# Block transposes by VectorE, gates on GpSimd and stores from ScalarE's queue in a fused chunk-selection attention and gated MLP kernel

## The chip, the cores and the metric

The kernel runs on one core of a Trainium2 chip. A core has five engines that run side by side, each through its own instruction list: TensorE (PE, matmuls; its weight loads are listed as PEld), VectorE (DVE), ScalarE (ACT), GpSimd (POOL) and SyncE (SP, here only the queue from which DMAs are issued). The metric is device microseconds for one execution: the median of three runs before the change is 215.47 us (215.21 to 215.66).

## What is computed

The reference is an attention that selects chunks of keys, followed by a gated MLP block that mixes tokens. Shapes: 4 batches, 8 heads, 768 tokens, head size 64; model width 512, inner width 1024.

```python
k_min, k_max = per-chunk min and max of k         # 24 chunks of 32 tokens
ub = sum_d max(q * k_min, q * k_max)              # bound of each query for each chunk
top_chunks = the 6 best chunks at or before the query's own
scores = q @ k.T / 8, kept where (j's chunk is in top_chunks) and j <= i
x = softmax(scores) @ v                           # [4, 768, 512], heads side by side
h = gelu(x @ w_in);  u, v = halves of h
v_n = layernorm(v) * g_ln
v_s = einsum('ts,bsd->btd', w_sg, v_n) + b_sg
out = x + (u * v_s) @ w_out
```

## The kernel before

**Pairs and batches.** Heads are worked in 16 pairs (pair p has heads 2p and 2p+1, four pairs to a batch). For each pair `prep` runs a K side, a q side, a V side and a selection; then come the scores with their exponentials, the products with V (`head`), and the transposed output (`xtrans`). When the fourth pair of a batch is done, `moe_h` and `moe_g` do the MLP for that batch, so that attention of later pairs and the MLP of an earlier batch lie in the same stretch of time.

**K side (`kside`, line 621).** `load_rows` (line 524) brings K of a pair as 128 tokens by 6 blocks by 2 heads by 64, two DMAs of 192 KB per tensor in runs of 256 B. TensorE transposes fp32 blocks of 128x128 against an identity (`rows_T`, line 545), six to a pair; VectorE reduces each transposed half to chunk minima and maxima straight from PSUM (line 643); ScalarE, and VectorE for pair 2, writes K as bf16 into `KA` (line 451). From pair 8 on (`KSPR`) both heads are written at once and two DMAs (lines 656 and 659) copy the second head to its own buffer and restore the mask rows there. GpSimd turns the maximum into maximum minus minimum (line 662).

**K side of pairs 12 to 15 (`kside2`, line 563, set `K2`).** GpSimd casts K to bf16 (line 572), two transposing DMAs write `KA` (line 576); VectorE transposes K in fp32 in blocks of 32x32 (line 579), reduces it (line 585), and every second pair regroups the results with 16 small copies (`regroup`, line 600). A transposing DMA and a copy ahead of pair 12 (`kb_init`, line 557) set up the constant rows.

**q side (`qside`, line 666).** Two groups of three fp32 transposes on TensorE, two evacuations into `qT` on ScalarE (VectorE for pairs 2 and 3), then on GpSimd the positive part (line 676) and bf16 casts into `QA` (line 683).

**Selection.** `select` (line 691) serves pairs 0 to 3, `select_full` (line 744) the later ones, two pairs at a time; `GROUPS` says which pairs go together. Small TensorE tiles give the bounds (lines 713 and 760), VectorE transposes them, takes the eight largest of each row, compares and transposes back. For later pairs four DMAs (line 793) put the result beside q.

**MLP.** `moe_h`: hidden products (lines 961 and 1007), GELU on ScalarE, batch statistics on VectorE, the power -1/2 of the variance on GpSimd (line 976), the normalization on VectorE (line 996). `moe_g`: token mixing on TensorE (line 1024), scale and bias on VectorE (line 1042), the gate product on VectorE (line 1046), the output matmul (line 1058), the residual (line 1066) and a store from SP's queue (line 1071) out of a ring of three buffers `osb`.

**Order.** Nothing is ordered at run time. `P.op` records each operation with its reads and writes; the table `TABLE` at the end lists, by operation number, the order in which each engine runs its operations and which PSUM slot each tile has; `link` derives the semaphore waits. A waiting instruction holds all that stands behind it on its engine, DMA issues among them.

## Time and profile before

| | |
|---|---|
| median of three runs | 215.47 us |
| span of the profiled execution, the only time that the profile gives for it | 216.2 us |
| VectorE busy | 187.7 us, 87% |
| ScalarE busy | 148.6 us, 69% |
| GpSimd busy | 106.1 us, 49% |
| DMA traffic | 36.26 MB, mean 168 GB/s |
| read from HBM, written | 24.77 MB, 6.29 MB |

The profile is of one execution. Busy times count the instructions that compute; issuing a DMA and waiting are not counted. Matmul ends are modelled, and overlapping matmuls are merged in busy time. A "chain" in the profile is followed back from the last instruction, at each step to what released it. Idle time of an engine matters only where another one waits for it.

### The profile page before, as it was taken

How to read it: one execution, taken by the hardware profiler on the slowest of the kernel's cores; microseconds unless marked ns; L12 is line 12 of the kernel's file. 1: busy time of each engine (PE TensorE's matmuls, PEld its weight loads, DVE VectorE, ACT ScalarE, POOL GpSimd, SP SyncE). 2: the span in 40 equal slices, each digit the busy share in tenths (PEclk: the TensorE clock that was granted, in tenths of full speed). 3: DMA queues.
4: the chain of work that ended last, by engine and by line, in shares of the span. 5: the costliest groups of instructions: out<-in, count | busy, mean ns of one | idle time of the engine just before them, and what ended most of it. 6: DMA issues, size and time to landing. Idle time of an engine off the chain costs nothing.

```text
span 216.2 us, 5890 instructions
## 1 busy us (share of the span) xinstructions
PE 199.7 (92%) x2292; PEld 133.3 (62%) x2307; DVE 187.7 (87%) x553; ACT 148.6 (69%) x223; POOL 106.1 (49%) x163
## 2 busy tenths in 40 slices
PE   7779998989999999999999997998796999999992
PEld 3547766745775668785466765875354686555650
DVE  3699997799999999998999999998997668788983
ACT  2768999847797597899478785998477597353000
POOL 7284669794539576655513936586531224011000
PEclk9999999999999999999999999999999799999998
DMA  7999999992789969948999899099731404501215
GB/s 153 219 219 180 245 326 234 346 289 63 167 224 236 203 149 245 209 122 195 227 184 204 203 172 263 22 183 199 155 60 40 112 0 40 181 0 53 97 75 216
DMA packets 95915, 36.26 MB, mean 168 GB/s; under 512 B 89488, under 2 KB 91024, under 8 KB 95888
## 3 DMA queue, kind: packets, MB, share of 16 engines
q1 hardware_dynamic: 95888, 35.89, 74.6%
q8 instruction: 18, 0.29, 0.6%
q14 instruction: 9, 0.07, 0.2%
HBM read 24.77 MB, written 6.29 MB: 144 GB/s over the span
## 4 chain that ended last, share of the span: by engine, by line
PE 74%; DVE 13%; ACT 5%; issue 2%; POOL 2%; DMA 2%; SPq 1%; DVEq 0%
PE PSG L1024 15%; PE PSC L834 11%; PE PSG L1058 8%; PE PSG L1007 7%; PE PSG L545 7%; PE PSG L961 6%; PE PSG L912 6%; PE PSG L760 3%; PE PSC L874 3%; DVE Wg L600 2%; PE PSG L919 2%; PE PSC L376 2%; DVE stats L970 2%; DMA out_dram<-osb 2%; PE PSC L880 2%
## 5 line engine op out<-in xcount | busy, mean ns | idle before, releaser
L840 ACT ACTIVATE E<-PSC 128x1024 bf16<-128x1024 f32 (+1 forms) x72 | 63.2, 921 | 14.5 <-PE PSC L834 13.5
L834 PE MATMUL PSC<-QA,KA 128*128 128x128 bf16 (+2 forms) x336 | 38.4, 248 | 2.5 <-ACT E L840 2.5
L1024 PE MATMUL PSG<-wsgT,vhat 128*128 128x384 bf16 x192 | 35.8, 334 | 0.2 <-DVE vhat L996 0.2
L683 POOL CAST QA<-qT 64x768 bf16<-64x768 f32 (+1 forms) x28 | 23.2, 835 | 16.8 <-ACT qT L451 12.3
L834 PEld LDWEIGHTS PSC<-QA,KA 128*128 128x128 bf16 x336 | 24.3, 99 | 11.0 <-ACT E L840 3.8
L845 POOL TENSOR_SCALAR_AFFINE_SELECT E<-E 128x768 bf16<-128x768 bf16 x24 | 20.6, 866 | 20.1 <-ACT E L840 20.0
L643 DVE TENSOR_REDUCE W<-PSG 128x12 f32<-128x384 f32 x48 | 24.3, 546 | 5.0 <-PE PSG L545 4.6
L1024 PEld LDWEIGHTS PSG<-wsgT,vhat 128*128 128x128 bf16 x192 | 18.5, 99 | 12.1 <-issue 0.8
L1012 ACT ACTIVATE uT<-PSG 128x384 bf16<-128x384 f32 x32 | 14.7, 491 | 15.5 <-PE PSG L1007 15.4
L1042 DVE SCALAR_TENSOR_TENSOR PSG<-PSG,glnT,bsgbc 128x384 f32<-128x384 f32 x32 | 19.5, 617 | 6.5 <-PE PSG L1024 6.2
L965 ACT ACTIVATE vgb<-PSG 128x512 f32<-128x512 f32 x24 | 14.0, 597 | 13.1 <-PE PSG L961 12.8
L1007 PE MATMUL PSG<-xT,winb 128*128 128x384 bf16 x128 | 22.8, 326 | 0.0
L961 PE MATMUL PSG<-winb,xT 128*128 128x512 bf16 x91 | 21.3, 379 | 1.4 <-DVE xT L454 1.1
L889 ACT ACTIVATE E<-PSC 128x1024 bf16<-128x1024 f32 (+1 forms) x24 | 20.7, 914 | 2.6 <-PE PSC L880 2.5
L1058 PE MATMUL PSG<-woutb,uT 128*128 128x512 bf16 (+1 forms) x90 | 21.8, 370 | 0.6
L912 PE MATMUL PSG<-vx,E 128*128 128x65 bf16 x480 | 20.0, 193 | 1.0 <-issue 0.8
L912 PEld LDWEIGHTS PSG<-vx,E 128*128 128x128 bf16 x480 | 17.7, 97 | 3.5 <-issue 1.1
L1066 DVE TENSOR_TENSOR osb<-PSG,XS 128x512 f32<-128x512 f32 (+1 forms) x25 | 16.2, 660 | 2.9 <-PE PSG L1058 1.6
L929 DVE TENSOR_TENSOR XS<-PSG,rden 128x384 bf16<-128x384 f32 x32 | 17.4, 551 | 0.5
L1046 DVE TENSOR_TENSOR uT<-PSG,uT 128x384 bf16<-128x384 f32 x32 | 17.2, 551 | 0.5
L451 ACT ACTIVATE qT<-PSG 128x384 f32<-128x384 f32 x28 | 13.6, 496 | 5.3 <-PE PSG L545 5.0
L1007 PEld LDWEIGHTS PSG<-xT,winb 128*128 128x128 bf16 x128 | 12.2, 98 | 8.1 <-ACT vgb L965 0.3
(93 smaller groups left out, 351.2 us busy)
## 6 DMA issues: line engine op xcount, KB each, us to landing
kn<-in_k_dram SPq DMA_DIRECT2D x32, 192.0 KB, 4.3
qn<-in_q_dram SPq DMA_DIRECT2D x32, 192.0 KB, 4.5
vn<-in_v_dram SPq DMA_DIRECT2D x16, 384.0 KB, 5.5
out_dram<-osb SPq DMA_DIRECT2D x23, 256.0 KB, 2.6
uT<-in_moe_w_sg_dram SPq DMA_DIRECT2D x4, 384.0 KB, 6.7
vgb<-in_moe_w_in_dram SPq DMA_DIRECT2D x3, 512.0 KB, 4.9
QA<-Dt SPq DMA_DIRECT2D x24, 36.0 KB, 2.0
vhat<-in_moe_w_sg_dram SPq DMA_DIRECT2D x2, 384.0 KB, 7.4
```

The lines of the kernel that those rows point to most:

```text
L643: P.op("dve", lambda d, m=m, op=op, src=src, h0=h0, h1=h1: d.tensor_reduce(W[w][:, m, 12 * h0:12 * h1].rearrange("p (h c) -> p h c", h=h1 ...
L683: P.op("pool", lambda g, i=i, r0=r0, r1=r1: g.tensor_copy(QA[w][i or 0][r0:r1, :], qT[r][r0:r1, :]), gps(S, 250 if i == 1 else 150), ("qca ...
L834: r = e.matmul(t.ap()[:, o:o + n], KA[w][i][:, 128 * kb:128 * kb + 128], QA[w][i][:, q0:q0 + n], start=True, stop=True)
L840: P.op("act", lambda e, t=t, c0=c0, c1=c1, i=i: e.activation(E[es][:, i, c0:c1], t.ap()[:, 0:c1 - c0], ACTF.Exp, scale=SCALE), act(c1 - c0 ...
L845: P.op("pool", lambda g, ev=ev: g.affine_select(ev, ev, pattern=[[0, NT], [1, 128]], compare_op=ALU.is_ge, fill=0.0, base=0, channel_multi ...
L889: P.op("act", lambda e, t=t, c0=c0, c1=c1, n=n: e.activation(E[es][:, :, c0:c1], t.ap().rearrange("p (i x) -> p i x", i=2)[:, :, 0:n], ACT ...
L912: r = e.matmul(t.ap()[:, 65 * qb:65 * qb + 65], E[es][:, i, a:a + 128], vx[w][:, kb, i, :], start=first, stop=False, skip_group_check=True)
L961: r = e.matmul(t.ap()[:, 0:F], xT[s][:, dk, 128 * qt:128 * qt + 128], winb[:, dk, F:DFF], start=(dk == 0), stop=(dk == NDK - 1))
L1007: r = e.matmul(t.ap()[:, 0:TG], winb[:, dk, 128 * fb:128 * fb + 128], xT[s][:, dk, TG * tg:TG * tg + TG], start=(dk == 0), stop=(dk == NDK ...
L1024: r = e.matmul(t.ap()[:, 0:TG], vhat[s][:, sb, 128 * fb:128 * fb + 128], wsgT[:, sb, TG * tg:TG * tg + TG], start=(sb == 0), stop=(sb == N ...
L1042: P.op("dve", lambda d, t=t, fb=fb, tg=tg: d.scalar_tensor_tensor(t.ap()[:, 0:TG], t.ap()[:, 0:TG], glnT[:, fb:fb + 1], bsgbc[:, TG * tg:T ...
L1058: r = e.matmul(t.ap()[:, 0:c1 - c0], gT[s][:, fb, 128 * qt:128 * qt + 128], woutb[:, fb, c0:c1], start=(fb == 0), stop=(fb == NF - 1))
```

## The change

- **K of pairs 8 to 15** (`KB`) and **q of pairs 9, 11, 13 and 15** (`QB`) are loaded by a new `load_slices`: four DMAs per tensor, one for each head and half of the head size, each onto 32 partitions in runs of 128 B, so that one VectorE transpose in blocks of 32x32 yields the transposed tensor as it is needed. For K that transpose goes to a scratch tile, from which VectorE takes minima and maxima of all 24 chunks, ScalarE copies the first head and VectorE the second head to `KA` as bf16 (`kblock`). For q it goes straight to `qT`. The set `K2` is empty, and with it go the transposing DMAs of K, the casts and the regrouping; for pairs 8 to 11 the copies of lines 656 and 659 go as well.
- **Gates** of batches 0, 1 and 2 (`GP`, all 24): VectorE writes scale and bias to SBUF in fp32 instead of back to PSUM, and GpSimd forms the product.
- **The power** is split in two halves of three token blocks (`RS = 2`).
- **Stores** of batches 0 to 2 are issued from ScalarE's queue (`STQ`); those of batch 3 stay on SP and come from the six buffers of `vgb` instead of the ring (`OSV`).
- **Selection**: pairs 2 and 3 form one group.
- **Order**: all lists of the table and the slots are written anew; matmuls that only keep TensorE warm at the start go from 12 to 7.

```diff
+    KB = (8, 9, 10, 11, 12, 13, 14, 15)
+    QB = (9, 11, 13, 15)
+    KBC = ("act", "dve")
...
+    RS = 2
+    STQ = (0, 1, 2)
...
+    OSV = (3,)
-    K2 = tuple(range(12, 16))
+    K2 = ()
...
-    GROUPS = [(0,), (1,), (2,), (3,)] + [(a, a + 1) for a in range(4, NP, 2)]
+    GROUPS = [(0,), (1,), (2, 3), (4, 5), (6, 7), (8, 9), (10, 11), (12, 13), (14, 15)]
...
+    def load_slices(p, nm, src, dst):
...
+        flat = dst[s][:].rearrange("p j i d -> p (j i d)").rearrange("p (c e) -> p c e", e=32)
+        for i in range(2):
+            for dh in range(2):
+                g = 2 * i + dh
+                o = P.op("sp", lambda e, i=i, dh=dh, g=g: e.dma_start(
+                    flat[32 * g:32 * g + 32], bass.AP(src.tensor, (2 * p + i) * S * DH + 32 * dh,
+                                                      [[DH, 32], [32 * DH, NC], [1, 32]])), dmac(),
...
+    def kblock(p):
...
+        P.op("dve", lambda d: d.transpose(KT, kn[s][:].rearrange("p j i d -> p (j i d)")), (865, 962), ("kbt", p),
+             reads=kr, writes=INDR)
+        for m, op in ((0, ALU.min), (1, ALU.max)):
+            P.op("dve", lambda d, m=m, op=op: d.tensor_reduce(
+                W[w][:, m, 0:NC], KT.rearrange("p (c x) -> p c x", x=32), axis=AX.X, op=op),
...
+            if KBC[i] == "act":
+                P.op("act", lambda e, i=i, r0=r0: e.activation(KA[w][i][r0:r0 + 64, :], KT[r0:r0 + 64, :], ACTF.Copy), (734, 845),
...
+        if p in QB:
+            P.op("dve", lambda d: d.transpose(qT[r][:], qn[s][:].rearrange("p j i d -> p (j i d)")), (865, 962), ("qbt", p),
...
+                if (b, k) in GP:
+                    xg = vgb[:, k % NT, 0:TG]
...
+                    P.op("dve", lambda d, t=t, fb=fb, tg=tg, xg=xg: d.scalar_tensor_tensor(
+                        xg, t.ap()[:, 0:TG], glnT[:, fb:fb + 1], bsgbc[:, TG * tg:TG * tg + TG],
...
+                    P.op("pool", lambda g, xg=xg, tg=tg, fb=fb: g.tensor_tensor(
+                        gT[s][:, fb, TG * tg:TG * tg + TG], xg, uT[s][:, fb, TG * tg:TG * tg + TG], op=ALU.mult),
...
-                    P.op("sp", lambda e, qt=qt, os_=os_, c0=c0, c1=c1: e.dma_start(
+                    P.op("act" if b in STQ else "sp", lambda e, qt=qt, ob=ob, c0=c0, c1=c1: e.dma_start(
```

## What was predicted before the changed kernel was run

> **What bounds the kernel now.** I read the page first, then the busy time by stretches, then the chain of waits, then the groups of instructions with shapes kept apart.
>
> ```profile
> span 216.2 us, 5890 instructions
> ...
> PE 199.7 (92%) x2292; PEld 133.3 (62%) x2307; DVE 187.7 (87%) x553; ACT 148.6 (69%) x223; POOL 106.1 (49%) x163
> ```
> ```profile
> 0.00:18.00 18.00, 14.33 (x121) 8.37 (x121) 12.15 (x44) 10.83 (x18) 9.93 (x26) 1.00 1.14 199
> 18.00:36.00 18.00, 17.90 (x349) 13.22 (x348) 16.88 (x57) 17.17 (x26) 13.18 (x20) 1.00 1.04 252
> 36.00:48.00 12.00, 10.09 (x185) 7.36 (x187) 9.29 (x36) 8.37 (x14) 10.52 (x16) 1.00 1.06 307
> 48.00:126.00 78.00, 77.41 (x818) 53.13 (x822) 74.49 (x211) 61.86 (x100) 45.37 (x64) 1.00 0.87 189
> 126.00:168.00 42.00, 36.09 (x474) 24.71 (x477) 38.41 (x136) 31.40 (x44) 20.59 (x34) 0.98 0.69 135
> 168.00:210.00 42.00, 41.74 (x347) 25.76 (x351) 34.23 (x71) 18.96 (x27) 6.50 (x8) 0.98 0.25 65
> 210.00:216.20 6.20, 2.16 (x12) 0.77 (x9) 2.25 (x5) 0.00 (x0) 0.00 (x0) 0.85 0.59 213
> ```
>
> Columns: length of the stretch, then busy time of PE, PEld, DVE, ACT and POOL with instructions in brackets, clock, DMA share, GB/s. PE is idle 16.5 us in all: 3.7 in the first 18 us (the first loads), 4.0 in the last 6 (the last addition and store), 1.9 in 36 to 48, 0.6 in the 78 us from 48 to 126, and 5.9 in 126 to 168. So from 48 to 126 and again in 168 to 210 the order of PE's own work is the time; VectorE is right behind it in the first of these (74.49 of 78 us) and is the cause of the gap in 126 to 168 (38.41 of 42). The chain shows this by name:
>
> ```profile
> 15.26 1.22 PE PSG L713 x18
> 21.34 1.22 PE PSG L713 x18
> 69.03 1.13 PE PSG L760 x32
> 122.33 0.36 PE PSG L545 x3
> 141.71 1.29 SPq L576
> 143.04 3.88 DMA out_dram<-osb
> 160.13 1.35 POOL rstd L976
> ```
> ```profile
> L643 DVE TENSOR_REDUCE W<-PSG 128x12 f32<-128x384 f32 x48 | 24.3, 546 | 5.0 <-PE PSG L545 4.6
> L451 ACT ACTIVATE qT<-PSG 128x384 f32<-128x384 f32 x28 | 13.6, 496 | 5.3 <-PE PSG L545 5.0 <-POOL QA L683 0.2
> L451 ACT ACTIVATE KA<-PSG 128x384 bf16<-128x384 f32 x14 | 6.9, 501 | 1.5 <-DVE W L643 1.5
> L1046 DVE TENSOR_TENSOR uT<-PSG,uT 128x384 bf16<-128x384 f32 x32 | 17.2, 551 | 0.5
> L840 ACT ACTIVATE E<-PSC 128x640 bf16<-128x640 f32 x24 | 16.9, 706 | 5.3 <-PE PSC L834 5.3
> L585 DVE TENSOR_REDUCE Wp<-IND 128x24 f32<-128x768 f32 x8 | 7.5, 934 | 0.0
> L600 DVE COPY Wg<-Wp 32x24 f32<-32x24 f32 x32 | 5.4, 169 | 0.4
> L579 DVE STREAM_TRANSPOSE IND<-kn 128x768 f32<-128x768 f32 x4 | 3.8, 955 | 0.0
> L805 DVE COPY KA<-INDF 64x768 bf16<-64x768 bf16 x8 | 3.1, 393 | 0.1
> L996 DVE TENSOR_SCALAR vhat<-vgb,mv,rstd 128x512 bf16<-128x512 f32 x24 | 11.4, 537 | 1.0 <-POOL rstd L976 0.8
> L662 POOL TENSOR_TENSOR W<-W 128x24 f32<-128x24 f32 x12 | 2.8, 238 | 5.0 <-DVE W L643 4.8
> L418 POOL TENSOR_TENSOR INDF<-IND 128x768 bf16<-128x768 bf16 x1 | 1.6, 1639 | 1.5 <-ACT IND L415 1.5
> L572 POOL CAST INDF<-kn 128x384 bf16<-128x384 f32 x4 | 2.0, 506 | 0.5 <-DMA KA<-INDF 0.4
> ```
>
> Columns of the chain: start, length, what, how many. Columns of the groups: line, engine, operation, shapes, count, busy us, mean ns of one, idle before. Between 126 and 168 us the chain is on DVE: the regrouping copies of line 600 (two bursts of 16, 5.4 us busy), reductions, batch statistics, then the power on POOL.
>
> **The change, part by part.** All sums are against the profiled execution's span, 216.2 us; the median of the three runs is 215.47, so I multiply by 0.9966 at the end. About 0.2% (0.43 us) is what a measurement of this kernel can tell from no change.
>
> *TensorE.* Block transposes replace 6 fp32 transposes for K of each of pairs 8 to 11 and for q of each of pairs 9, 11, 13 and 15: 48 matmuls. The chain's row has three of them in 0.36 us, 0.12 each: minus 5.8 us. 36 of them (4.3 us) lie in 48 to 126, the others behind. K of pairs 12 to 15 was not on PE before. Pairs 2 and 3 are selected together: two runs of line 713 at 1.22 us become one, and the paired run of line 760 (1.13) is nearest to it: minus 1.2 us, in 18 to 36 where PE is full (17.90 of 18). If pair 2's mask, which now waits for pair 3's K and q, comes late, this gain is gone, so it lies between 0 and 1.2. PE's busy time goes to 192.7.
>
> *VectorE.* Removed: the 32 copies of line 600, 5.4 us; 24 gate products of line 1046 at 0.55, 13.2 us; for pairs 8 to 11, 16 reductions of line 643 at 0.546, 8.7 us. Added: the transpose of line 579 (0.955) for four more K and four q, 7.6 us; 8 reductions of line 585 (0.934), 7.5 us; 8 copies of half a KA, 64x768 f32 to bf16. The trace has no such copy: line 805 moves 64x768 from bf16 in 0.393, line 996 makes bf16 from 512 f32 in 0.537, or 0.81 for 768, so 3.1 to 6.5 us; I take 0.5 each, near line 805, 4.0 us. Four more small additions before the power cost under 1 us. In all minus 8 us, but unevenly. In 48 to 126 it loses 12 to 16 gates (6.6 to 8.8 us) and gains 1.14 for each of pairs 8 to 11 (0.955 + 2 x 0.934 - 4 x 0.546 + 0.5) and two q, 6.5 us: almost nothing. VectorE at 95% thus becomes the cover over PE's 4.3 us there; 74.5 us less about 1 of work, packed nearly as PE is now (0.6 idle), would need some 75.5 of the 78 us, so I credit 2.5 and lose 1.8. In 126 to 168 it loses line 600's 5.4 us and some three gates (1.6), and gains two q (1.9) and four copies (2.0): minus 3.1.
>
> *The waits in 126 to 168.* Before the store at 143.04 stands a transposing DMA of 1.29 us on SP's queue; the next addition into that buffer waited:
>
> ```profile
> 147.02 0.69 DVE L1066 TENSOR_TENSOR osb<-PSG,XS 128x512 f32<-128x512 f32 x1 [0.95 <-DMA out_dram<-osb]
> ```
> ```profile
> 143.04 0.58 SPq L1071 DMA_DIRECT2D out_dram<-osb  x1
> ```
>
> The transposing DMAs of K are gone, so this store issues earlier and the 0.95 us of VectorE goes; the ring of three output buffers stays for batches 0 to 2. The power in two halves lets the first three normalizations start early; one half costs between 0.67 and 1.35 us. Of PE's 5.9 us of idle time I take 3.5 to go (3.1 of work and part of the 0.95); next in line are the statistics and the softmax on ScalarE, which stay.
>
> *GpSimd.* 24 products of 128x384. Lines 662 and 418 (24 and 768 columns, 0.238 and 1.639 us) give 0.92 by a straight line; 0.55 (VectorE's) is the lower end and 1.64 the upper; 0.92 it is, as both rows are products of two inputs on this engine: 22 us, against 4.0 us less for the casts of line 572. POOL ends near 123 us.
>
> *ScalarE.* It loses 8 evacuations of K (0.50) and 8 of q (0.50), 8 us, and gains 8 half KA of 64x768, 0.81 each from line 840's 640 columns, 6.5 us. And it issues 18 stores, each 0.58 us on SP's row: 10.4 us in its instruction order, with the exponentials queued behind. It has 42 - 31.40 and 42 - 18.96 us free where batches 1 and 2 store. SP's queue loses these 18, nine transposing issues (1.29) and eight mask copies, and gains 24 loads, so nothing behind it comes later.
>
> *New waits of PE.* The output matmuls of batches 0 to 2 now wait in six places for the last gate on POOL, 0.92 instead of 0.55: 2.2 us if nothing covers it, half of that since score and transpose matmuls stand between: 1.1. Stores on ScalarE: 0.4. Together 1.5.
>
> *DMA.* Twelve tensors are loaded in 3072 runs of 128 B instead of 1536 of 256 B, nine transposing DMAs go.
>
> ```profile
> DMA packets 95915, 36.26 MB, mean 168 GB/s; under 512 B 89488, under 2 KB 91024, under 8 KB 95888
> ```
> ```profile
> DMA packets 10420, 2.63 MB, mean 219 GB/s; under 512 B 10419, under 2 KB 10419, under 8 KB 10419
> ```
> ```profile
> DMA packets 38138, 12.00 MB, mean 182 GB/s; under 512 B 36470, under 2 KB 37334, under 8 KB 38128
> ```
> ```profile
> QA<-Dt SPq DMA_DIRECT2D x24, 36.0 KB, 2.0
> glnT<-in_moe_g_ln_dram SPq DMA_DIRECT2D x1, 2.0 KB, 2.3
> ```
>
> From 6 to 18 us nothing but 256-byte runs moves: 12 us x 16 engines / 10420 = 18.4 ns a run. A tensor is 1.77 us of all engines. Under 512 B the page counts 89488 packets; less 73728 for K, q and V and 512 for the gain vector, 953 are left for each of 16 transposing DMAs (seven of XS, nine for K), 9.9 us for nine. If a 128-byte run costs r of a 256-byte one, the change adds 42.4 r - 31.1 us. The bounds: glnT with 32 runs of 4 B per engine lands 0.3 us after QA with two, 10 ns a run, r = 0.54 (a gain of 8 us of traffic); r = 1 adds 11.3. In 84 to 150, where these loads lie, 182 of 219 GB/s leave 11.2 us free. I take r = 0.75, between, nearer to the run without bytes: 0.7 us, hidden, as all is up to r = 1.
>
> [...]
>
> *Sum:* 216.2 - 5.8 - 1.2 + 1.8 - 3.5 + 1.5 = 209.0, or 208.3 as a median. With its unknowns, not all at one end at once (waits 0 to 4, idle 0 to 5.9, pair 2's 1.2, the 1.8), the forecast alone lies between 202.5 and 212.5.
>
> **The rivals.** *VectorE binds.* Its 95% in 48 to 126 stays, all 4.3 us of PE there turn into idle time and only 1 us of the later gap goes: 216.2 - 7.0 + 4.3 - 1.0 + 1.5 = 214.0, median 213.3. For it: the stretch's DVE sum hardly moves. Against: the order is written anew.
>
> *ScalarE's queue.* Six stores of batch 0 fall where ScalarE is full:
>
> ```profile
> 82.00:102.00 20.00, 19.61 (x326) 15.36 (x327) 18.04 (x58) 17.92 (x26) 11.79 (x17) 1.00 0.83 188
> ```
> ```profile
> 60.00:90.00 30.00, 29.80 (x350) 20.94 (x351) 28.16 (x80) 23.05 (x35) 20.86 (x31) 1.00 0.90 210
> 114.00:144.00 30.00, 28.37 (x392) 21.35 (x393) 29.35 (x85) 24.31 (x33) 18.92 (x29) 1.00 0.87 171
> ```
>
> 17.92 of 20 us, and six issues are 3.5: 209.0 + 3.5, median 211.8.
>
> *Gates late on POOL, slower than before.* In 60 to 90 POOL is busy 20.86 of 30 us; eight gates at 0.92 make 28.2, and from 1.14 us a gate it is over-full. Diagonal masks and q casts then stand between the gates, and PE, in order, waits at each of the six groups of output matmuls. Without the 1.1 the sum is 207.9; slower than 216.2 from 1.4 us a wait; with 2.0 us, two such instructions ahead, it is 219.9, median 219.2. Against: in 114 to 144 the sum is 18.92 + 7.4, and batch 2 has more room.
>
> *The short runs.* If r were 1.17 or more, 7.3 us beyond the free 11.2 would eat the gain of 7.2; at 1.5 it is 21.3 - 7.2 = 14 us slower, median 229.5. Such a price needs a shorter run to cost more than a longer one; the bound from glnT speaks against it, and the 256-byte runs reach 219 GB/s, but no row has 128-byte runs into SBUF, so it stays open. [...]
>
> **How the numbers follow.** Forecast 0.62; VectorE binds 0.12 (0.04 of it within 0.2%); ScalarE's queue 0.08; gates late 0.13 (0.03 within, 0.10 slower); short runs 0.05. Faster 0.62 + 0.08 + 0.08 = 0.78, same 0.07, slower 0.15. The range 202.5 to 215.0 takes in the forecast, the ScalarE and the VectorE case, and leaves out the slower cases and half of those within 0.2%, some 2 in 10.
>
> **What would show it.** Right: PE busy near 193; no line-600 group; PE idle in the stretch before batch 2's token mixing near 2 us instead of 5.9; DVE near 180; POOL near 123 with gate products of 0.8 to 1.0 us; K and q loads of 128 B landing before the transpose needs them, with DVE's transposes showing no idle time released by a load. Wrong: PE waiting on POOL's products at the output matmuls, exponentials late behind stores, DVE's transposes released by loads, or PE idle in 48 to 126 of 4 us or more.

## The result and the profile after

The changed kernel takes 212.03 us (median of four runs, 211.54 to 214.74), the kernel before 215.35 (215.21 to 215.66) beside it: ratio 0.9838, 95% interval 0.9814 to 0.9862. It is faster by 3.3 us; the forecast had 7.2. The slowest of the four, 214.74 us, had a lowered granted clock (0.992) and is left out of the ratio, which by itself makes the gain 3.5 us. The profiled execution shown ahead of the prediction had a lowered TensorE clock from 126 us on (0.98, 0.98 and 0.85 in its rows; span 216.2 us); another execution of the same kernel at full clock, e1 below, has a span of 213.9 us, and it is the one compared here. The two spans compared differ by 4.2 us where the medians differ by 3.3, so differences read from these two traces are good to about 1 us.

The page of the changed kernel, its span and the engines:

```profile
span 209.7 us, 5781 instructions
...
PE 193.1 (92%) x2254; PEld 125.7 (60%) x2254; DVE 185.0 (88%) x507; ACT 155.5 (74%) x221; POOL 126.9 (61%) x179
```

The same stretches as before (columns as in the prediction: length, then PE, PEld, DVE, ACT and POOL with instructions in brackets, clock, DMA share, GB/s):

```profile
18.00:36.00 18.00, 15.99 (x331) 11.80 (x326) 16.75 (x48) 15.89 (x24) 15.24 (x21) 1.00 1.12 265
36.00:48.00 12.00, 10.12 (x201) 7.70 (x198) 11.28 (x28) 9.42 (x14) 8.94 (x12) 1.00 0.80 213
48.00:126.00 78.00, 75.30 (x808) 49.95 (x807) 77.22 (x213) 65.94 (x97) 56.15 (x77) 1.00 0.97 181
126.00:168.00 42.00, 39.21 (x504) 25.80 (x502) 35.82 (x110) 38.82 (x50) 26.07 (x34) 1.00 0.52 101
```

And of the kernel before at full clock:

```profile
18.00:36.00 18.00, 17.89 (x349) 13.21 (x348) 16.89 (x57) 17.17 (x26) 13.16 (x20) 1.00 1.02 250
36.00:48.00 12.00, 10.60 (x187) 7.65 (x189) 9.77 (x40) 8.87 (x14) 11.01 (x17) 1.00 1.09 313
48.00:126.00 78.00, 77.41 (x818) 53.19 (x822) 74.56 (x206) 61.84 (x100) 44.52 (x62) 1.00 0.85 188
126.00:168.00 42.00, 36.26 (x482) 25.12 (x485) 38.84 (x138) 32.01 (x44) 21.62 (x36) 1.00 0.70 142
```

TensorE's idle time in 126 to 168 went from 5.74 to 2.79 us, about as forecast. But it grew from 0.59 to 2.70 in 48 to 126, where the forecast had allowed some 2.4 (0.6 and the 1.8 for VectorE's cover), and from 0.11 to 2.01 in 18 to 36, where it had allowed nothing. The chain of the changed kernel tells the same in one line, its shares of the span by engine:

```profile
PE 39%; DVE 36%; DMA 11%; ACT 5%; issue 4%; SPq 3%; DVEq 0%; POOL 0%
```

and that of the kernel before at full clock:

```profile
PE 74%; DVE 13%; ACT 5%; issue 2%; POOL 2%; DMA 2%; SPq 1%; DVEq 0%
```

TensorE was three quarters of the path and is less than half of it now; VectorE and landings of DMAs came in. The list of what TensorE waits for (total us, times, longest) shows many waits of about 1 us, ended by VectorE, landings of DMAs, ScalarE and GpSimd:

```profile
PE PSG L1015 <- DVE vhat L987: 1.4, 1, 1.4
PE PSC L860 <- DVE Dt L726: 1.4, 1, 1.4
PE PSC L820 <- DMA QA<-Dt: 1.4, 2, 0.8
...
PE PSG L998 <- DMA xT<-XS: 1.2, 1, 1.2
PE PSG L572 <- ACT KA L461: 1.0, 1, 1.0
PE PSG L513 <- DVE XS L915: 1.0, 1, 1.0
PE PSG L746 <- POOL rT L662: 0.9, 1, 0.9
```

The kernel before has about as many such waits, the longest of them these two, but in its list no wait is ended by a DMA; in the changed kernel such waits add up to 3.1 us.

```profile
PE PSC L834 <- ACT E L840: 1.5, 1, 1.5
PE PSG L760 <- DVE rden L927: 1.5, 1, 1.5
```

Where in time the gain lies is read from the first hidden product of `winb` with `xT` in each batch's MLP, line 961 before and 947 after (start, length, line). The kernel before at full clock:

```profile
45.71 1.46 PE L961 MATMUL PSG<-winb,xT 128*128 128x512 bf16 x6 [0.88 <-DVE xT L454]
...
99.00 0.81 PE L961 MATMUL PSG<-winb,xT 128*128 128x512 bf16 x3 [0.22 <-DVE xT L454]
...
148.50 0.81 PE L961 MATMUL PSG<-winb,xT 128*128 128x512 bf16 x3 [0.77 <-DVE XS L929]
...
183.61 0.59 PE L961 MATMUL PSG<-winb,xT 128*128 128x512 bf16 x2
```

The changed kernel:

```profile
47.36 0.82 PE L947 MATMUL PSG<-winb,xT 128*128 128x512 bf16 x3 [0.79 <-DVE xT L464]
...
96.26 0.81 PE L947 MATMUL PSG<-winb,xT 128*128 128x512 bf16 x3
...
145.26 1.03 PE L947 MATMUL PSG<-winb,xT 128*128 128x512 bf16 x4
...
180.38 0.81 PE L947 MATMUL PSG<-winb,xT 128*128 128x512 bf16 x3 [0.57 <-DVE osb L1072]
```

Batch 0 starts 1.7 us later than before, batch 1 is 2.7 us earlier, batches 2 and 3 are 3.2 us earlier, and the end is 4.2 us earlier (213.9 to 209.7). So the front lost, and the stretch between batches 0 and 1 is 4.4 us shorter. Not all of that is gain: 33 of the 48 transposes that went lay in this stretch, but the changed order also puts eight output matmuls of batch 0 (line 1060) behind its end and 12 transposes of `wsb` (line 513) ahead of its start.

Cut at batch 0's mark, the two executions read, first the kernel before:

```profile
0.00:45.71 45.71, 40.94 (x642) 28.19 (x643) 36.63 (x118) 35.69 (x53) 31.93 (x57) 1.00 1.07 247
45.71:213.87 168.16, 157.51 (x1651) 104.56 (x1664) 151.11 (x436) 112.97 (x170) 74.13 (x107) 1.00 0.66 149
```
```profile
0.00:47.36 47.36, 39.98 (x648) 27.47 (x649) 40.58 (x121) 35.95 (x53) 33.73 (x59) 1.00 1.05 230
47.36:209.70 162.34, 153.07 (x1606) 98.20 (x1606) 144.39 (x387) 119.58 (x168) 93.22 (x121) 1.00 0.69 141
```

In the front TensorE's busy time fell by 1.0 us and its idle time rose by 2.6 (4.77 to 7.38). Behind it the kernel is 5.8 us shorter.

Some groups of the changed kernel that the prediction had priced (count, busy us, mean ns):

```profile
L1040 POOL TENSOR_TENSOR uT<-vgb,uT 128x384 bf16<-128x384 f32 x24 | 22.4, 947 | 9.5 <-DVE vgb L1036 9.3
L965 POOL TENSOR_TENSOR rstd<-rstd,neghalf 128x3 f32<-128x3 f32 x8 | 7.3, 916 | 24.9 <-DVE rstd L963 24.8
L987 DVE TENSOR_SCALAR vhat<-vgb,mv,rstd 128x512 bf16<-128x512 f32 x24 | 13.9, 619 | 1.1 <-POOL rstd L965 1.1
L791 DVE COPY KA<-INDF 64x768 bf16<-64x768 bf16 x8 | 6.2, 780 | 0.1
```

The gates cost what was forecast (0.947 against 0.92 us). The last two are old work that became slower: the normalization took 537 ns before, the copy of the mask rows 393. The slow ones (four of the 24 normalizations, 912 to 1101 ns, and six of the eight copies, 707 to 1093) stand beside casts and diagonal masks on GpSimd, which the kernel before has too, and not beside the gates.

### The profile page after: what moved, and what is told of

Its sections match the earlier page's. It is cut to its first block, busy times and chain, and to the rows that moved or that the text cites. A ratio compares the mean times of both kernels' runs of the same rounds, so it can differ in the third digit from the quotient of the medians.

```text
span 209.7 us, 5781 instructions
## 1 busy us (share of the span) xinstructions
PE 193.1 (92%) x2254; PEld 125.7 (60%) x2254; DVE 185.0 (88%) x507; ACT 155.5 (74%) x221; POOL 126.9 (61%) x179
## 2 busy tenths in 40 slices
DMA packets 106891, 33.71 MB, mean 161 GB/s; under 512 B 100976, under 2 KB 102000, under 8 KB 106864
## 4 chain that ended last, share of the span: by engine, by line
PE 39%; DVE 36%; DMA 11%; ACT 5%; issue 4%; SPq 3%; DVEq 0%; POOL 0%
PE PSG L1015 8%; PE PSG L947 6%; PE PSG L1060 5%; PE PSG L998 5%; PE PSC L820 5%; DMA QA<-Dt 5%; DVE m L766 4%; DVE U L755 3%; DVE W L619 3%; DVE vgb L1036 3%; DVE XS L915 3%; DMA bsgbc<-in_moe_b_sg_dram 3%; DVE KA L791 3%; PE PSG L572 3%; PE PSG L898 2%
## 5 line engine op out<-in xcount | busy, mean ns | idle before, releaser
L1015 PE MATMUL PSG<-wsgT,vhat 128*128 128x384 bf16 x192 | 34.5, 326 | 1.4 <-DVE vhat L987 1.4
L820 PEld LDWEIGHTS PSC<-QA,KA 128*128 128x128 bf16 x336 | 23.6, 98 | 12.3 <-ACT E L826 4.5
L1040 POOL TENSOR_TENSOR uT<-vgb,uT 128x384 bf16<-128x384 f32 x24 | 22.4, 947 | 9.5 <-DVE vgb L1036 9.3
L998 PE MATMUL PSG<-xT,winb 128*128 128x384 bf16 x128 | 23.7, 326 | 1.2 <-DMA xT<-XS 1.2
L1060 PE MATMUL PSG<-woutb,uT 128*128 128x512 bf16 (+1 forms) x100 | 23.7, 370 | 0.0
L947 PE MATMUL PSG<-winb,xT 128*128 128x512 bf16 x96 | 22.2, 379 | 1.4 <-DVE xT L464 0.8
L965 POOL TENSOR_TENSOR rstd<-rstd,neghalf 128x3 f32<-128x3 f32 x8 | 7.3, 916 | 24.9 <-DVE rstd L963 24.8
L619 DVE TENSOR_REDUCE W<-PSG 128x12 f32<-128x384 f32 x32 | 16.1, 544 | 3.8 <-POOL W L395 2.7
L1036 DVE SCALAR_TENSOR_TENSOR vgb<-PSG,glnT,bsgbc 128x384 f32<-128x384 f32 x24 | 14.3, 605 | 5.3 <-PE PSG L1015 5.2
L956 DVE BATCH_NORM_STATS2 stats<-vgb 128x6 f32<-128x512 f32 x24 | 15.7, 678 | 2.2 <-ACT vgb L951 2.1
```

Of the source, the lines that this page charges most:

```text
L619: P.op("dve", lambda d, m=m, op=op, src=src, h0=h0, h1=h1: d.tensor_reduce(W[w][:, m, 12 * h0:12 * h1].rearrange("p (h c) -> p h c", h=h1 ...
L820: r = e.matmul(t.ap()[:, o:o + n], KA[w][i][:, 128 * kb:128 * kb + 128], QA[w][i][:, q0:q0 + n], start=True, stop=True)
L947: r = e.matmul(t.ap()[:, 0:F], xT[s][:, dk, 128 * qt:128 * qt + 128], winb[:, dk, F:DFF], start=(dk == 0), stop=(dk == NDK - 1))
L998: r = e.matmul(t.ap()[:, 0:TG], winb[:, dk, 128 * fb:128 * fb + 128], xT[s][:, dk, TG * tg:TG * tg + TG], start=(dk == 0), stop=(dk == NDK ...
L1015: r = e.matmul(t.ap()[:, 0:TG], vhat[s][:, sb, 128 * fb:128 * fb + 128], wsgT[:, sb, TG * tg:TG * tg + TG], start=(sb == 0), stop=(sb == N ...
L1040: P.op("pool", lambda g, xg=xg, tg=tg, fb=fb: g.tensor_tensor(gT[s][:, fb, TG * tg:TG * tg + TG], xg, uT[s][:, fb, TG * tg:TG * tg + TG], ...
```

## The experiments

All ratios are to the kernel before, run beside it on the same chip. Two kernels that did not run beside each other are compared by their ratios, turned into us with 215.35.

**The base, and one part undone at a time (e1 to e4).** e1 is the kernel before, unchanged.

> The kernel before, unchanged. The four executions of the changed kernel have 2.1 us around their span, and the median of before is 215.35, so theory A (the profiled execution of before, with a granted clock of 0.88 and 0.84 between 162 and 174 us, was not like the timed ones) expects a span near 213.2 us with the clock at 1.0 throughout, matmul groups shorter than before by what the clock took (line 1024 at 326 ns instead of 334), and PE's idle time between 126 and 168 us still above 4 us. The rival, that 216.2 is the usual span, expects 216 us again with the clock dip.

Measured: 215.69 us, ratio 1.0002 (0.9967 to 1.0037); span 213.9 at clock 1.00. The idle time of 126 to 168 was real (5.74 us) and some 2.3 us of the 216.2 were the clock.

e2 puts the gates back on VectorE, in places worked out for them in the changed kernel's order:

```diff
-    GP = [(0, 0), (0, 1), ..., (2, 7)]
+    GP = []
```

> The changed kernel with its 24 gate products on VectorE as before, right behind scale and bias; everything else and the rest of the order kept. [...] The rival, that the late gates on GpSimd are what TensorE waits for, expects the time to stay or fall below 212.

Measured: 221.21 us, ratio 1.0235 (1.0179 to 1.0291).

```profile
PE 195.5 (89%) x2242; PEld 126.5 (58%) x2254; DVE 194.4 (89%) x531; ACT 155.8 (71%) x221; POOL 105.5 (48%) x155
```

Without the gates' move the change, in this order, is slower than the kernel before, where the rival expected the changed kernel's 212 us or less: the move is worth 8.5 us here (1.0235 against 0.9838). TensorE waits 5.2 us for the gate products on VectorE (line 1048), 3.3 of them at line 898; in the changed kernel it waits for no gate. What an order written for gates on VectorE would cost was not run. The normalizations stay at a mean of 616 ns with a longest of 1092 (619 and 1101 in the changed kernel), the comparison of line 771 at a longest of 1359 (1357), so it isn't the gates that hold them.

e3 loads the sliced tensors in runs of 256 bytes, with the same number of DMAs and bytes; rows come in another order, so the values of these K and q are not the reference's.

```diff
-    flat[32 * g:32 * g + 32], bass.AP(src.tensor, (2 * p + i) * S * DH + 32 * dh,
-                                      [[DH, 32], [32 * DH, NC], [1, 32]])
+    <32 partitions, 12 runs of 64>, bass.AP(src.tensor, (2 * p + i) * S * DH + 32 * DH * dh,
+                                      [[DH, 32], [64 * DH, NC // 2], [1, DH]])
```

> The changed kernel whose sliced loads (K of pairs 8 to 15, q of 9, 11, 13, 15) bring the same bytes with as many DMAs in runs of 256 B instead of 128 B; it leaves out that the tokens stand where the block transpose needs them, so its numbers are others, its work is the same. Theory C (the 18432 more packets make the small DMAs of the selection and the transposing DMAs of the output late; they are on the chain for 11% of the span) expects about 88500 packets, QA from Dt landing in 2.0 us instead of 2.5 and XS into xT in 3.1 instead of 4.4, and 1 to 3 us less time than the changed kernel. The rival, that the short runs are hidden, expects a time within 0.4 us of the changed kernel.

Measured: 213.13 us, ratio 0.9878 (0.9826 to 0.9930), with 88459 packets instead of 106891: no gain. Nor did the small transfers land sooner: `QA` from `Dt` took a median of 2.4 us (2.5 in the changed kernel), `XS` into `xT` 4.4 as before.

e4 issues the 18 stores from SP again, each placed by its time in that queue:

```diff
-    STQ = (0, 1, 2)
+    STQ = ()
```

> The changed kernel with its 18 stores of batches 0 to 2 issued from SP's queue again, each placed by its time in that queue. ScalarE's issues took 0.34 us each in the changed kernel, 6.1 us in all, with exponentials behind them. Theory D (they hold ScalarE where it is full) expects 1 to 3 us less time than the changed kernel; the rival, that SP's queue would hold loads behind waiting stores, expects 0.5 to 3 us more; if ScalarE's issues are covered, the time stays within 0.4 us.

Measured: 213.54 us, ratio 0.9890 (0.9811 to 0.9969). The interval holds the changed kernel's 0.9838: the queue of the stores can't be told from no difference.

**The front (e5, e6, e9).** e5 selects pairs 2 and 3 one after the other again.

```diff
-    GROUPS = [(0,), (1,), (2, 3), (4, 5), ...
+    GROUPS = [(0,), (1,), (2,), (3,), (4, 5), ...
```

> The changed kernel with pairs 2 and 3 selected one after the other again, as in the kernel before; the rest of each engine's order is kept, the few new instructions stand where their inputs are ready. Theory A (selecting pairs 2 and 3 together is what cost the front): TensorE's idle time in 18 to 36 us, 2.01 in the changed kernel and 0.11 in the kernel before, falls below 1.0, and the kernel is 0.8 to 1.5 us faster than the changed one, ratio to the kernel before 0.977 to 0.981. Rival B (the time at the front is paid for later anyway, by VectorE, which is busy 77 of the 78 us from 48 to 126): the idle time in 18 to 36 falls too, but that of 36 to 126 (4.6 in the changed kernel) rises by about as much, and the ratio stays at 0.984 within 0.003. Rival C (the grouping is not the cause, the loads are): the idle time in 18 to 36 stays at 2.

Measured: 211.99 us, ratio 0.9837 (0.9778 to 0.9897).

```profile
PE 195.0 (93%) x2254; PEld 127.1 (61%) x2254; DVE 183.4 (88%) x508; ACT 155.5 (74%) x221; POOL 126.4 (60%) x179
```
```profile
18.00:36.00 18.00, 17.20 (x337) 12.90 (x335) 16.51 (x53) 16.21 (x25) 14.58 (x20) 1.00 1.13 265
```

These are the page's engines and the stretch of 18 to 36 us. TensorE's idle time there falls from 2.01 to 0.80, as A and B had it, but over the whole span its busy time rises by 1.9 with the run of bounds that comes back, and nothing is gained in the sum. (The interval leaves room for 1.3 us either way.) Batch 0's first hidden product comes at 46.69 us instead of 47.36, so the pairing explains less than half of the late front. B had the time right and not the way: it isn't VectorE that takes the gain later (TensorE's idle time in 36 to 126 is 4.8 us against 4.6). The pairing took a run off TensorE and paid for it with as much waiting.

e6 has ScalarE write the mask rows, and e9 has VectorE set the same rows to zero (the masks' rows are left out):

```diff
-    P.op("dve", ... d.tensor_copy(KA[w][i][m0:m0 + 64, :], INDF[m0:m0 + 64, :])
+    P.op("act", ... d.activation(KA[w][i][m0:m0 + 64, :], INDF[m0:m0 + 64, :], ACTF.Copy)
```
```diff
-    d.tensor_copy(KA[w][i][m0:m0 + 64, :], INDF[m0:m0 + 64, :])
+    d.memset(KA[w][i][m0:m0 + 64, :].bitcast(mybir.dt.uint32), 0)
```

> The changed kernel with VectorE's ten copies of the mask rows (64x768, 342 to 1093 ns each, 6.2 us in all against 3.1 before) done by ScalarE instead, at 0.7 to 0.85 us each as its block copies; the order of the rest is kept. Theory A (the holds of these copies beside GpSimd's work delay VectorE's chain of selections at the front): VectorE's busy time falls by 6, TensorE's idle time in 18 to 48 (3.9) falls by 1 to 2, and the kernel is about 1 us faster than the changed one, ratio about 0.979. Rival B (what GpSimd holds up is passed on: the next VectorE instruction is held instead, and ScalarE has 7 us more work in a stretch where the masks are waited for): the median time of comparisons and normalizations stays, their maxima too, and the ratio is 0.984 to 0.988.

> The changed kernel in which VectorE's ten copies of the mask rows into KA (64x768, 6.2 us in the first 47 us, 2.7 in the kernel before) are memsets of the same rows; the masks' rows are left out, so that the output isn't the reference's. Order and waits are kept. Theory A (the front is late because GpSimd holds these copies: the first matmul of batch 0's input product stands at 47.4 us, in the kernel before at 45.7): a memset, which reads nothing, takes 0.35 to 0.4 us and is not held, VectorE is 2.5 to 3 us shorter in the front, the first input product starts at 46 or earlier, and the whole time falls by 1.0 to 1.7, ratio 0.976 to 0.979. Rival B (the front is late for its loads and for TensorE's order; VectorE waits elsewhere for what it gains): the first input product stays at 47 and the ratio at 0.982 to 0.986. Rival C (a memset is held like a copy): the memsets' longest are 0.9 us or more, and nothing moves.

(There are eight such copies, not ten as these two texts say.) Measured: e6 213.12 us, ratio 0.9883 (0.9831 to 0.9935); e9 212.29, ratio 0.9846 (0.9766 to 0.9926). The instructions' shortest, median and longest ns are, in the changed kernel and in e9:

```profile
L791 DVE COPY KA<-INDF x8: 342/906/1093, 22.1 to 43.2; 64x768 bf16<-64x768 bf16 x8
```
```profile
L791 DVE MEMSET KA<- x8: 378/378/378, 23.3 to 43.1; 64x384 uint32 x8
```

The copies were held, the memsets are not, and VectorE is 3.2 us shorter for it. The front does not gain by it: batch 0's first hidden product stands at 47.7 us instead of 47.4. So theory A of e9 falls and its rival B stands; the ratio alone, whose interval reaches down to 0.9766, could not tell them apart. In e6 VectorE is 6.7 us shorter, ScalarE is busy 17.68 of 18 us in 18 to 36, and the front is no earlier either (48.7 us).

**The order (e7, e8).** Both kernels with the same instructions in an order of mine:

```diff
-    "pe": (  <the order of each kernel>
+    "pe": (  "1 43 47 52 54 77 81 59 86 88 100 104 186 192 ...   (the kernel before)
+    "pe": (  "1 54 52 47 43 77 81 59 86 88 104 100 182 93 ...    (the changed kernel)
```

> The kernel before with the same instructions, of which only the order on each engine, the buffers they use and the place of the eight idle matmuls at the start are written out anew. It tells what an order alone is worth, so that the changed kernel's parts and its order can be told apart. Theory A (the kernel before was bound by TensorE's sum, 199 of 214 us busy, and an order can only take from its 15 us of idle time): TensorE's busy time stays at 198 to 199, its idle time falls from 15 to 10 to 12, and the time is 210.5 to 212.5, ratio 0.977 to 0.987: as much as the whole change brought. Rival B (the idle time belongs to the waits for loads and for VectorE, whatever the order): 215 to 216, ratio 0.998 to 1.002.

> The changed kernel with the same instructions, of which only the order on each engine and the buffers they use are written out anew. Theory A (the change's parts took 5.4 us off TensorE, from 198.5 to 193.1, and its order gave part of it back as idle time, 16.6 against 15.4): with another order the idle time falls to 11 to 13, 126 to 168 us included, and the time is 206 to 208, ratio 0.957 to 0.966, some 4 us under the kernel before in its new order. Rival B (VectorE's time, 185 of 209.7 with the holds by GpSimd, is what sets the time from 48 to 126 whatever the order): the idle time there stays at 2.5 to 3, VectorE at 99% of that stretch, and the time is 210 to 212, ratio 0.975 to 0.984.

Measured: 223.30 us, ratio 1.0346 (1.0291 to 1.0401), and 219.72, ratio 1.0188 (1.0127 to 1.0248). Both expectations of a gain were wrong: an order alone moved either kernel by some 7.5 us, for the worse. In e8 the idle matmuls of the start, tied to one instruction, fell between the first transposes, and batch 0's first hidden product came at 52.4 us instead of 47.4. Still the two differ by 0.0158, 3.4 us, as they do in their own orders, with an uncertainty of some 1.8 us. These are two orders written apart, one for each kernel, so this only makes it unlikely that the gain is the order's alone.

**VectorE's and ScalarE's added work (e10 to e12).** e10 cuts the block transposes and reductions of pairs 8 to 11 and the four transposes of q to 32 columns, so that most of these K and q is not computed:

```diff
+    z = 32 if p < 12 else 768
-    d.transpose(KT, kn[s]...)
+    d.transpose(KT[:, 0:z], kn[s]...[:, 0:z])
...
-    d.transpose(qT[r][:], qn[s]...)
+    d.transpose(qT[r][:, 0:32], qn[s]...[:, 0:32])
```

> The changed kernel in which the block work that VectorE gained is cut to one block of 32 columns: the transposes and both reductions of K for pairs 8 to 11, and the transposes of q for pairs 9, 11, 13 and 15. The rest of these K and q is not computed, so the output isn't the reference's; order and waits are kept. VectorE loses 8 x 0.85 + 8 x 0.83, some 13 us, nine of them in 48 to 126. Theory A (VectorE, busy 77.2 of 78 us there, has become the bound): TensorE's idle time in 48 to 126 falls from 2.7 to under 1, and the whole falls by 2 to 5 us, ratio 0.960 to 0.975. Rival B (TensorE in its written order is the bound there still, and waits for loads and for ScalarE): VectorE's time falls by 13, the whole by less than 1, ratio 0.980 to 0.986.

Measured: 213.71 us, ratio 0.9894 (0.9814 to 0.9974).

```profile
PE 192.5 (91%) x2242; PEld 126.1 (60%) x2254; DVE 174.5 (83%) x507; ACT 155.5 (74%) x221; POOL 127.2 (60%) x179
```
```profile
48.00:126.00 78.00, 74.90 (x802) 49.82 (x806) 68.31 (x215) 65.49 (x97) 56.65 (x77) 1.00 0.88 175
```

VectorE falls from 77.22 to 68.31 of 78 us in that stretch, and TensorE gains nothing from it (74.90 us busy against 75.30). What TensorE waits for has only changed its name: in e10's list of waits two small transfers come first.

```profile
PE PSC L821 <- DMA QA<-Dt: 2.7, 4, 1.5
PE PSG L999 <- DMA xT<-XS: 2.0, 1, 2.0
```

e11 and e12 put the exponential in the place of the Gelu, in the changed kernel and in the one before, so that 13 of 14 and 7 of 8 table loads go; the activation of the MLP is another one then.

```diff
-    ACTF.Gelu_apprx_tanh
+    ACTF.Exp
```

> The changed kernel with the exponential in place of its Gelu, so that ScalarE needs one table and 13 of its 14 table loads (1.283 us each) go, 16.7 us of ScalarE; the output isn't the reference's, order and waits are kept. Beside it stands the kernel before with the same edit, which loses 7 of 8 loads, 9.0 us. Theory A (the six loads more than before are on the path: ScalarE is busy 38.8 of 42 us in 126 to 168, in the kernel before 32.0): the changed kernel falls by 1.5 to 4 us more than the kernel before does; ratio 0.96 to 0.972 here. Rival B (they lie beside other work): both fall by about the same, under 1.5 us.

> The kernel before with the exponential in place of its Gelu (seven of its eight table loads go, 9.0 us of ScalarE; the output isn't the reference's). Theory A (the table loads the change added are on the path, those of before hardly): 0 to 1.5 us faster, ratio 0.993 to 1.0, against 1.5 to 4 more of the changed kernel. Rival B (table loads cost both kernels the same): the fall here, in us, is that of the changed kernel within 0.8.

Measured: 212.80 us, ratio 0.9835 (0.9762 to 0.9908), and 215.59, ratio 0.9976 (0.9929 to 1.0022). ScalarE is 16 us shorter in e11 (139.3 against 155.5) and the time is that of the changed kernel, within the interval's 1.6 us. Rival B holds: with all else in place, the six loads that the new order added lie beside other work.

**What a transpose is worth in either kernel (e13, e14).** The transposes of q of pairs 8, 10, 12 and 14 are done three times, 48 more matmuls of the kind that the change removed, with the same output:

```diff
-    P.op("pe", rows_T(qn[s], t, hf), ...
+    P.op("pe", lambda e, f=rows_T(qn[s], t, hf): [f(e) for _ in range(3 if p in (8, 10, 12, 14) else 1)][-1], ...
```

> The changed kernel with the transposes of q of pairs 8, 10, 12 and 14 done three times over: 48 matmuls more on TensorE, as many as the change took away, the same output. By the profile's mean of 0.16 us each (TensorE's union time for the transposes fell by 6.8 to 7.8 us for 48) they are 7 to 8 us. Theory A (TensorE in its written order is the time, and a matmul taken from it is worth its whole length): 219 to 220, ratio 1.015 to 1.022, that is, slower than the kernel before; then the transposes were worth 7 to 8 and the change's other parts lost 4. Rival B (half of it is absorbed by waits that other engines end): 214.5 to 216.5, ratio 0.995 to 1.005, and the removal was worth no more than the 3.3 us measured.

> The kernel before with the same 48 transposes more (q of pairs 8, 10, 12 and 14 three times over), same output. Theory A: 7 to 8 us slower, ratio 1.032 to 1.038. Rival B (half absorbed): 3 to 4.5 us slower, ratio 1.014 to 1.021. If the two kernels differ in this, the kernel with the smaller rise is the one whose TensorE waits for others.

Measured: the changed kernel 214.12 us, ratio 0.9916 (0.9888 to 0.9944), so 0.0078 or 1.7 us more than without them; the kernel before 222.25, ratio 1.0297 (1.0233 to 1.0362), 6.4 us more. The group of these transposes in the kernel before, with them and in e1 without:

```profile
L545 PE MATMUL PSG<-identF,qn 128*128 128x128 f32 x144 | 20.7, 277 | 0.7 <-ACT KA L451 0.7
```
```profile
L545 PE MATMUL PSG<-identF,qn 128*128 128x128 f32 x96 | 15.4, 279 | 0.7 <-ACT KA L451 0.7
```

48 of them take 5.3 us. In the kernel before they cost their whole length (5.0 to 7.8 us by the interval; the one execution of e14 with a granted clock of 1.00, 220.68 us, lies 5.2 above the mean of the kernel before's at that clock); in the changed kernel a third of it, 0.9 to 2.5 us. In e13 TensorE is busy 197.0 us and idle 14.2, against 193.1 and 16.6: waits took up part of the added work. Both results lie outside the ranges that the two texts gave, which had taken a transpose for 0.16 us. This is the plainest line between the two kernels: before, TensorE was the bound in the middle of the kernel; after, it isn't. The theory that it still is (A of e13, 219 to 220 us) falls.

**All of it at once, and the loads (e15 to e18).** e15 has the edits of e9, e10 and e11 and cuts each gate on GpSimd to 32 of 384 columns; e16 has the runs of 256 bytes of e3 besides; e17 has only the edits of e10 and e3; e18 keeps everything, but each sliced load fetches 6 of its 24 column blocks. In all four, parts of K, q, masks, gates or activations are left out or changed as described.

```diff
-    gT[...][TG * tg:TG * tg + TG], xg, uT[...][TG * tg:TG * tg + TG]
+    gT[...][TG * tg:TG * tg + 32], xg[:, 0:32], uT[...][TG * tg:TG * tg + 32]
```
```diff
-    flat[32 * g:32 * g + 32], ... [[DH, 32], [32 * DH, NC], [1, 32]]
+    flat[32 * g:32 * g + 32, 0:6], ... [[DH, 32], [32 * DH, 6], [1, 32]]
```

> The changed kernel with all its added work beside TensorE cut at once: the block transposes and reductions of pairs 8 to 11 and of four q to 32 columns, memsets for the mask copies, the gates on GpSimd to 32 of 384 columns, one table on ScalarE. These parts of the computation are left out, so the output isn't the reference's; TensorE's instructions, loads, order and waits are those of the changed kernel. VectorE falls by 14, ScalarE by 16, GpSimd by 19 us. Theory A (the engines hide behind each other: where one is cut, the next ends the same wait): the time falls by 3 to 6 us, ratio 0.957 to 0.970, TensorE's idle time from 16.6 to 11 to 13. Rival B (TensorE's order and the landing of small transfers set the time): 210.5 to 212.5, ratio 0.977 to 0.987.

> The same as the kernel with all of the added work cut, with the sliced loads in runs of 256 bytes besides (rows in another order, so that their values aren't the reference's). Theory A (the loads and the landing of small transfers behind them are the next limit, once the engines are out of the way): another 1.5 to 3 us faster than without this edit, and the landing of the regrouped masks (2.5 us median) and of the transposing copies into xT (4.4) falls towards the kernel before's 2.1 and 3.3. Rival B: within 1 us of the kernel without this edit.

> The changed kernel with the block transposes and reductions of pairs 8 to 11 and the transposes of four q cut to 32 columns, and the sliced loads in runs of 256 bytes; gates, mask copies and tables as in the changed kernel. The rest of these K and q is not computed and rows come in another order, so the output isn't the reference's. Theory A (VectorE's block work and the short runs are two bounds side by side, after which TensorE waits for whichever is later): 208 to 209.5, ratio 0.965 to 0.973, near the 208.4 of the kernel with all engines cut and long runs. Rival B (VectorE is not the partner; the tables or the gates are): 211.5 to 213, ratio 0.981 to 0.988.

> The changed kernel in which each sliced load of K and q (pairs 8 to 15) fetches 6 of its 24 column blocks, in 128-byte runs as before: 27648 packets fewer in the sliced loads, everything that the engines do and wait for in place; the values of these K and q are partly those of earlier pairs, so the output isn't the reference's. Theory A (the loads are one of two bounds side by side; the other, VectorE with its 77 of 78 us, still stands): 211 to 213, ratio 0.978 to 0.988, though the regrouped masks land in under 2.3 us instead of 2.5. Rival B (the loads are the one bound that counts and longer runs were too mild a cut): 207 to 209.5, ratio 0.960 to 0.972.

| kernel | us | ratio (interval) |
|---|---|---|
| e15, all engines' added work cut | 212.00 | 0.9811 (0.9752 to 0.9870) |
| e16, the same and 256-byte runs | 208.41 | 0.9673 (0.9610 to 0.9736) |
| e17, VectorE's blocks cut and 256-byte runs | 211.55 | 0.9818 (0.9763 to 0.9873) |
| e18, a quarter of the sliced loads | 213.17 | 0.9887 (0.9836 to 0.9938) |

The engines of e15 and of e16, in this order:

```profile
PE 194.4 (91%) x2254; PEld 126.4 (59%) x2254; DVE 171.2 (80%) x507; ACT 139.2 (65%) x208; POOL 109.9 (52%) x179
```
```profile
PE 191.2 (93%) x2254; PEld 125.4 (61%) x2254; DVE 170.0 (82%) x507; ACT 139.0 (67%) x208; POOL 109.9 (53%) x179
```

With 14 us of VectorE, 16 of ScalarE and 17 of GpSimd cut, the time stays; with most of the sliced loads cut and all engines in place, it stays (the regrouped masks land in 1.9 us instead of 2.5, so the cut did reach them). Only both together bring 3.6 us against the changed kernel. The simplest reading is that the loads and the engines stand side by side, and the later of the two ends TensorE's wait. e15 goes by its rival B. e16 goes by A in time (3.0 us between the ratios of e15 and e16, at the upper edge of the 1.5 to 3 expected) and only in part by its way: `xT` lands in 3.7 us instead of 4.3, but the regrouped masks in 3.0 instead of 2.6. TensorE's waits for these two fell from 5.7 us in e15 to 2.5, all for the masks. e18 goes by A too, just above the upper edge of its range. e17 goes by its rival B and tells that VectorE's block work isn't the loads' only partner: with it out of the way and long runs, the kernel is at 211.6, not near 208.4. Which of GpSimd's gates, ScalarE's table loads and the mask copies is the other partner was not told apart. Of the kernels that compute everything, none was faster than the changed one; e5 is equal to it.

## Why the prediction was wrong in its size

The direction and the range held; more than half of the gain did not come. Two terms of the sum failed. One is the credit for TensorE's matmuls at their full length: "The chain's row has three of them in 0.36 us, 0.12 each: minus 5.8 us", of which only 1.8 were given back for VectorE. The other is the front, where the sum had "minus 1.2 us" for pairs 2 and 3 and no new wait.

- **TensorE, minus 5.8 and plus 1.8.** The matmuls did go: the K and q transposes are 120 instead of 168, TensorE's busy time is 193.1 where 192.7 was forecast. (That they are so close is partly luck: the sum started from 199.7 at the lowered clock. At full clock it fell from 198.5, by 5.4 instead of 7.0.) But e13 and e14 show that the same work put back costs 6.4 us in the kernel before and 1.7 in the changed one. So beside the change's other parts the 48 transposes were worth 1.7, not the 4.0 credited: 2.3 us too much. The kernel before without them, which would tell what they are worth alone, was not run.
- **Pairs 2 and 3, minus 1.2.** The prediction named the condition, "If pair 2's mask, which now waits for pair 3's K and q, comes late, this gain is gone", and took the wrong end. TensorE waited 1.4 us for `Dt` of line 726, and e5 shows a gain of nothing. 1.2 us too much.
- **The idle time in 126 to 168, minus 3.5, and new waits, plus 1.5.** The idle time fell by 2.95. All that is left of the measured 3.3, once 1.7 for the transposes and nothing for the pairs are taken out, is 1.6, where these two terms made 2.0. Added up, 2.3, 1.2 and 0.4 are the 3.9 us between the forecast's 7.2 and the measured 3.3. It is an account by differences whose intervals are about 1 us each, it charges the transposes as the last part of the change, and the transposes that were put back are q's of the neighbouring pairs, near the place of those removed.
- **The same by time.** The marks split it otherwise. The forecast put batch 0 some 1.2 us earlier and the rest 6.0 shorter (5.8 and 3.5, less 1.8 and 1.5); batch 0 came 1.7 us later, and the rest is 5.8 shorter. The two spans fall 3.0 us short of 7.2, and 2.9 of these are short in the front. But a gain there need not last: in e5 batch 0 comes 0.7 us earlier and the end does not. So both terms were too good; how the shortfall divides between them stays open, and so does what, beside the pairing, made the front late. It isn't the mask copies (e6, e9).
- **VectorE binds (chance 0.12, 213.3 us).** Its time came closer than the forecast's, its reason did not hold: it had 4.3 us of new idle time of TensorE in 48 to 126, and 2.1 came. VectorE is at 99% in 48 to 126, and e10 takes 9 us of it out of that stretch without any gain. It can be one of several bounds at about the same height, and 99% busy did not make it the bound.
- **The loads.** "0.7 us, hidden, as all is up to r = 1" is right by e3, and silent on what comes next: by e15 and e16 the loads are a limit once the engines' added work is out of the way. The sliced loads of K and q themselves are not late, as no block transpose of VectorE waits for one. The fear that a run of 128 bytes costs more than one of 256 is answered by a stretch of the changed kernel full of these loads, 84 to 110 us:

```profile
DMA packets 23499, 4.88 MB, mean 188 GB/s; under 512 B 22983, under 2 KB 23111, under 8 KB 23495
```

  26 us of 16 engines over 23499 packets of all sizes are 17.7 ns a packet at most, not above the 18.4 of 256-byte runs. The trace's packet records of that stretch have 14569 packets of 128 B with a median of 13 ns and 7885 of 256 B with a median of 20: by these r is about 0.65, and the 0.75 taken was somewhat too high.
- **Gates late and ScalarE's queue.** Neither came. The gates took 0.947 us, TensorE waited for none of them, and in this order the change has its gain only with them on GpSimd (e2). The 211.8 us of ScalarE's queue is the nearest of all to the measured time, but by luck: e4 takes the stores off ScalarE and gains nothing. They cost 0.34 us each there where I had taken SP's 0.58:

```profile
L1078 ACTq DMA_DIRECT2D out_dram<-osb x18: 338/338/452, 93.5 to 201.3; - x18
```
- **VectorE's busy time, minus 8.** It fell by 2.7 (187.7 to 185.0). The missing 5.3 us are for the most part old work that the change did not touch and the prediction did not price: the held mask copies (3.1 to 6.2 us) and the normalizations (11.4 to 13.9). By e9 the held mask copies cost VectorE 3 us and the kernel nothing that shows; what the normalizations cost was not tested.
- **The signs.** Nearly all that was named for "right" came (no group of line 600, gates of 0.95 us, 2.79 us idle in 126 to 168, no transpose waiting for a load; VectorE at 185 instead of 180), and none of those for "wrong". No sign watched the first 48 us or asked what TensorE's work would still be worth, and it is there that the two terms failed.

## What to carry to other kernels

A bound resource pays the full price for work taken from it only until the next one is reached; with engines at 92, 88 and 74% and the DMA engines at 97% in 48 to 126 us that is soon, so ask of each term of the sum what would be late next if it came true in full. A cheap test of it is to put a piece of the removed work back: here 48 transposes cost their length (6.4 us) where that engine was the bound, and a third of it (1.7) where it wasn't. And work cut on one resource at a time shows nothing when two stand at the same height; cut them together before calling either one innocent.

## What the runs showed of the hardware

- VectorE's copies of 64x768 from bf16 to bf16 took 309 to 746 ns in the kernel before (its profile ahead of the prediction) and 342 to 1093 in the changed one, both with GpSimd at work beside them; in e9 memsets of the same bytes took 378 ns each time. The time went with which began first. Eight copies, six of the changed kernel's and two of the kernel before's, began while a cast or a mask ran on GpSimd, and each ended 0.21 us after it: the six took 707 to 1093, the two 746 and, where the mask had only 0.15 us to go, 366. Three of the kernel before's, beside which GpSimd's work began only after them, took 342 to 357. So the copies that came second were held, by up to 0.75 us (1093 less 342), and the memsets in their places weren't.
- TensorE's matmuls were longer at the start: in the kernel before the idle ones on `warm` took 634 ns each up to 5.3 us (the first 610) and 379 from 6.2 us on, the transposes of line 545 421 up to 5.9 us and some 273 from 6.1 on; in the changed kernel the transposes took 418 up to 6.2 us and 273 from 6.7 on. In e8, where TensorE had one idle matmul at 1.24 us and its next work at 5.49, three transposes still took 0.85 us at 6.82, against 0.55 at 10.53 us in the changed kernel. The slow part lasted longer where less work stood ahead; no run leaves the idle matmuls out.
- A store's issue took a median of 338 ns on ScalarE's queue and of 552 on SP's (at most 1396), when the same 18 stores were issued there among the loads (e4). The last batch's seven stores, behind all loads, took a median of 332 on SP, so the longer time isn't SP's as such.
- The same instructions in one other order took some 7.5 us more, in either kernel (e7, e8): more than twice what the whole change gained.
